# An attention block and a two-of-eight expert layer on one core: experts computed only on the rows routed to them, gathered and summed through DRAM

## The chip, the cores and the metric

The kernel runs on one core of one Trainium2 chip. Its engines are TensorE (PE in the profile, PEld for its weight loads), VectorE (DVE), ScalarE (ACT), GpSimd (POOL) and SyncE (SP). SP and ACT issue DMAs through hardware queues, POOL through a software queue. The metric is the time of the launch in device microseconds.

## The reference

All is float32. A linear attention with a polynomial sketch gives x, 4352 tokens of 128 values; a router picks two of eight experts for each token, and the output is the sum of the two experts' results, weighted by their gates.

```python
def phi(x):                                   # S1, S2: (8, 32)
    a = np.einsum('rd,bhsd->bhsr', S1, x); b = np.einsum('rd,bhsd->bhsr', S2, x)
    return np.einsum('bhsi,bhsj->bhsij', a, b).reshape(*x.shape[:-1], r * r)
kv = np.einsum('bhsf,bhsd->bhfd', phi(k), v); z = np.sum(phi(k), axis=2)
x = num / den                                 # num = phi(q) kv, den = phi(q) z; batch 4, heads 4, seq 1088
noisy_logits = x @ w_gate + np.log1p(np.exp(x @ w_noise)) * noise
top2 = np.argpartition(-noisy_logits, 2, axis=1)[:, :2]      # top2_w: softmax over the two
for e in range(E):                            # E = 8, w1[e]: (128, 1024), w2[e]: (1024, 128)
    for k in range(2):
        mask = top2[:, k] == e
        h = np.maximum(x[mask] @ w1[e], 0.0)
        out[mask] += top2_w[mask, k, None] * (h @ w2[e])
```

## The kernel before, in words

A batch has 1088 tokens, that is 8 tiles of 128 and a rest of 64; the rests of two batches share a tile. `attention(b)` loads k, v and q of a batch (SP), makes the keys (`key_values`: transposes at line 224, sketches at 191, the product on VectorE at 185, the sum over tokens at 240 and 242), lets POOL write each pair of heads of q twice (`twice`, line 256), and then works on two groups of four tiles: `queries` (transposes at 267, sketches at 272 and 273, products at 277, times the keys' sums at 286) and `router` (transposes of x at 305, logits at 310, some 30 small VectorE operations from 328 to 367). The router ends in the weight of every expert for every token, zero for six of eight. These weights are transposed on TensorE (371), stored to DRAM as (expert, token) by POOL (375) and read back spread over all partitions (395).

`experts` computes all eight experts for all 512 tokens of a group: x times the spread weight (398), w1 (402), ReLU on VectorE or ScalarE in turn (406, 408), w2 (389), all experts summed in one bank of PSUM. All weights, 8 MB, are loaded once (178, 179) and stay in SBUF. Then the sum is transposed back and stored (454, 456). There are eight groups of 512 tokens and one of 256, the rests. Batch 0's attention comes first; from then on each batch's attention is written ahead of the experts of two earlier groups.

The order on each engine is set when the kernel is built: a scheduler sorts the instructions of each engine, and attention's instructions stand between those of earlier groups' experts. Every engine takes its list in order. Tiles come from pools of a few buffers, and whoever writes a buffer waits until the last reader of its earlier content is done; a DRAM tile is one such object, so a write to it waits for the write before.

Of the kernel before, what the change touches and what calls it, by code (L numbers as in the profile page):

```python
# [16 lines left out]
# The largest float32 whose exp is finite.  # L17
# [4 lines left out]
def kernel(  # L22
# [22 lines left out]
    # A batch is NT full tiles of 128 tokens, token NT * p + t in row p of tile t, and a rest  # L45
    # of 64; the rests of two batches share a tile.
# [3 lines left out]
    G = 4  # L50
# [4 lines left out]

    const = ctx.enter_context(tc.tile_pool(name="const", bufs=1))
# [3 lines left out]
    keep = ctx.enter_context(tc.tile_pool(name="keep", bufs=2 * NG + 1))  # L60
    moe = ctx.enter_context(tc.tile_pool(name="moe", bufs=2))
    hpool = ctx.enter_context(tc.tile_pool(name="hpool", bufs=4))
    dram = ctx.enter_context(tc.tile_pool(name="dram", bufs=2 * NG + 1, space=DRAM))
# [50 lines left out]
    # Keys: rows (h, d), columns (h, sketch, r), a block for each head; the high and the low part.  # L114
# [6 lines left out]
    # Queries, for two heads: rows (part, h, d), columns (h, i, j), the i-th row of the first  # L121
    # sketch or the j-th of the second.
# [13 lines left out]
    # E for the first expert down to 1 for the last: of equal logits the first is taken.  # L136
# [26 lines left out]
    w1 = const.tile([P, E, F], F32, name="w1")  # L163
    w2 = const.tile([P, E, FJ, D], F32, name="w2")
# [12 lines left out]
    def load_weights(e):  # L177
        nc.sync.dma_start(w1[:, e, :], moe_w1[e])
        nc.sync.dma_start(w2[:, e, :, :], moe_w2[e].rearrange("(j p) d -> p j d", p=P))

# [119 lines left out]
    def router(x, n, t0):  # L300
        """x transposed, and every expert's weight of each token, in DRAM as (expert, token)."""
# [4 lines left out]
        xT = keep.tile([P, 512], F32, name="xT", tag="xT")  # L306
# [18 lines left out]
        # log(1 + exp(z)) = max(z, 0) + log(1 + u), u = exp(-|z|), with what 1 + u rounds off.  # L325
# [11 lines left out]
        # Where exp(z) overflows the reference's scale is infinite: one that outweighs all others.  # L337
# [6 lines left out]
        # The two largest, each one expert even among equals.  # L344
# [19 lines left out]
        gate = t3("gate")  # L364
        V.tensor_mul(out=gate, in0=first[0], in1=wide(g1))
        V.tensor_mul(out=c, in0=first[1], in1=wide(g2))
        V.tensor_add(out=gate, in0=gate, in1=c)  # L367
# [4 lines left out]
        gT = small.tile([E, 512], F32, name="gT", tag="gT")  # L372
        nc.vector.tensor_copy(gT[:, 0:w], ps[0:E, 0:w])
        gd = dram.tile([E, 512], F32, name="gd", tag="gd")
        nc.gpsimd.dma_start(gd[:, 0:w], gT[:, 0:w])
        return xT, gd

# [1 line left out]
    turn = [0]  # L379

    def experts(xT, gd, n):
        """The weighted experts of a group of tokens, as (token, D) in tiles of 128."""
        w = P * n
        acc = ps_o.tile([P, 512], F32, name="acc", tag="acc")
        EH = E // 4
        todo = []

        def second(e, j, h):
            nc.tensor.matmul(acc[:, 0:w], lhsT=w2[:, e, j, :], rhs=h[:, 0:w],  # L389
                             start=(e == 0 and j == 0), stop=(e == E - 1 and j == FJ - 1))  # L390

        for e0 in range(0, E, EH):
            # The weights are not negative: relu(w1 (g x)) = g relu(w1 x).
            gb = moe.tile([P, EH, 512], F32, name="gb", tag="gb")
            nc.gpsimd.dma_start(gb[:, :, 0:w], gd[e0:e0 + EH, 0:w].partition_broadcast(P))  # L395
            xg = moe.tile([P, EH, 512], F32, name="xg", tag="xg")
            for e in range(EH):
                nc.vector.tensor_mul(out=xg[:, e, 0:w], in0=gb[:, e, 0:w], in1=xT[:, 0:w])  # L398
            for e in range(e0, e0 + EH):
                for j in range(FJ):  # L400
                    hp = ps_h.tile([P, 512], F32, name="hp", tag="hp")
                    nc.tensor.matmul(hp[:, 0:w], lhsT=w1[:, e, P * j:P * (j + 1)],  # L402
# [8 lines left out]
                    if len(todo) > 2:  # L411
                        second(*todo.pop(0))
# [90 lines left out]
```

## Time and profile before

| | us |
|---|---|
| median of 2 runs (1117.38 to 1117.74) | 1117.56 |
| profiled execution, its span | 1118.2 |
| PE busy | 1066.1 |
| DVE busy | 327.1 |
| ACT busy | 230.8 |
| POOL busy | 46.4 |

The span runs from the first to the last instruction of one profiled execution. Busy times of different engines overlap. PE and PEld overlap as well, and a matmul's recorded duration is longer than the time by which it moves its successor, so rates are read from starts. A granted clock of 1.00 is TensorE's upper level, 2.4 GHz, and 0.50 the lower, 1.2 GHz.

### The profile page before, as it was taken

What the parts mean: (1) busy time and instruction counts of PE and PEld (TensorE: products, weight loads), DVE (VectorE), ACT (ScalarE), POOL (GpSimd) and SP (SyncE); (2) the same over time, 40 slices, a digit from 0 to 9 for tenths busy, and PEclk for the clock granted to TensorE, in tenths of its full rate; (3) what the DMA queues carried; (4) which work ended last, traced back from release to release, by engine and by line L of the source; (5) the groups of instructions that cost most, each with busy time, mean ns of one, the idle gap of its engine ahead of it and who ended that gap; (6) DMA issues with size and microseconds to landing.
All of it is one profiled execution on the core that took longest, in us unless ns stands there. A gap on an engine that the chain in (4) does not pass through costs nothing.

```text
span 1118.2 us, 8232 instructions
## 1 busy us (share of the span) xinstructions
PE 1066.1 (95%) x3072; PEld 535.6 (48%) x3072; DVE 327.1 (29%) x761; ACT 230.8 (21%) x406; POOL 46.4 (4%) x99
## 2 busy tenths in 40 slices
PE   1869999999999999999999999999999999999997
PEld 1636544444446444444455444444444444444586
DVE  2144442222223522222224522222223222222222
ACT  0123321111122311111113311111122111111221
POOL 2011100000000100000000000000000000000000
PEclk9969999999999999999999999999999999999999
DMA  8911000000000000000000000000000000000000
GB/s 209 317 45 51 21 1 23 26 25 27 22 24 5 20 19 19 28 20 19 20 29 0 21 20 19 29 19 19 19 29 19 19 20 28 10 10 10 19 1 6
DMA packets 29159, 35.95 MB, mean 32 GB/s; under 512 B 8056, under 2 KB 22656, under 8 KB 29120
## 3 DMA queue, kind: packets, MB, share of 16 engines
q1 hardware_dynamic: 17280, 16.91, 4.9%
q0 software_dynamic: 5216, 17.97, 4.8%
q10 hardware_dynamic: 6624, 0.56, 0.4%
q8 instruction: 24, 0.39, 0.1%
q14 instruction: 15, 0.12, 0.0%
HBM read 33.06 MB, written 2.37 MB: 32 GB/s over the span
## 4 chain that ended last, share of the span: by engine, by line
PE 89%; DVE 5%; DMA 2%; ACT 2%; issue 1%; ACTq 0%; POOL 0%; DVEq 0%
PE acc L389 39%; PE hp L402 39%; PE bank L272 2%; PE bank L240 2%; PE bank L191 2%; PE bank L273 1%; PE bank L286 1%; ACT L331 1%; PE bank L267 1%; DVE h L406 1%; PE bank L310 1%; DMA gb<-gd 1%; PE bank L371 0%; DMA words<-in_S_dram 0%; DMA rest_q<-in_q_dram 0%
## 5 line engine op out<-in xcount | busy, mean ns | idle before, releaser
L402 PE MATMUL hp<-xg,w 128*128 128x512 f32 (+1 forms) x1152 | 561.3, 569 | 0.0
L389 PE MATMUL acc<-h,w 128*128 128x512 f32 (+1 forms) x1152 | 558.7, 569 | 0.0
L406 DVE TENSOR_SCALAR h<-hp 128x512 f32<-128x512 f32 (+1 forms) x288 | 190.5, 662 | 608.9 <-PE hp L402 608.9
L389 PEld LDWEIGHTS acc<-h,w 128*128 128x128 f32 x1152 | 216.8, 190 | 235.4 <-issue 229.6
L402 PEld LDWEIGHTS hp<-xg,w 128*128 128x128 f32 x1152 | 215.9, 190 | 231.0 <-issue 227.7
L408 ACT ACTIVATE h<-hp 128x512 f32<-128x512 f32 (+1 forms) x288 | 165.0, 573 | 687.3 <-PE hp L402 687.3
L395 POOL DMA_DIRECT2D gb<-gd x36 | 20.1, 557 | 800.4 <-DVE xg L398 751.2
L398 DVE TENSOR_TENSOR xg<-gb,xT 128x512 f32<-128x512 f32 (+1 forms) x72 | 44.4, 654 | 2.4 <-DMA gb<-gd 2.4
L191 PE MATMUL bank<-sk,kT 128*128 128x64 f32 x136 | 20.1, 318 | 8.1 <-ACT kT L226 7.5
L277 DVE TENSOR_TENSOR phq<-qa,bank 128x512 f32<-128x512 f32 (+1 forms) x18 | 11.8, 658 | 44.6 <-PE bank L273 43.1
L191 PEld LDWEIGHTS bank<-sk,kT 128*128 128x128 f32 x136 | 19.9, 233 | 10.2 <-ACT kT L226 8.7
L272 PE MATMUL bank<-qT,sq 128*128 128x512 f32 (+1 forms) x36 | 21.8, 690 | 2.8 <-ACT qT L270 2.8
L286 PEld LDWEIGHTS bank<-kv,phq 128*128 128x128 f32 (+1 forms) x144 | 17.6, 186 | 9.4 <-DVE phq L277 4.0
L240 PE MATMUL bank<-vaug,phk 128*128 128x66 f32 x128 | 19.0, 311 | 3.0 <-DVE phk L185 3.0
L371 PE MATMUL bank<-ident,gate 128*8 128x128 f32 x34 | 5.6, 287 | 16.3 <-DVE gate L367 16.3
L240 PEld LDWEIGHTS bank<-vaug,phk 128*128 128x128 f32 x128 | 18.4, 226 | 5.0 <-DVE phk L185 3.2
L270 ACT COPY qT<-bank 128x512 f32<-128x512 f32 (+1 forms) x18 | 10.1, 562 | 49.7 <-PE bank L267 49.7
L273 PE MATMUL bank<-qT,sq 128*128 128x512 f32 (+1 forms) x36 | 20.0, 641 | 0.0
L286 PE MATMUL bank<-kv,phq 128*128 128x66 f32 (+1 forms) x144 | 17.2, 265 | 0.5 <-DVE phq L277 0.5
L185 DVE TENSOR_TENSOR phk<-kab 128x2048 f32<-128x2048 f32 x4 | 9.2, 2293 | 18.8 <-ACT kab L184 18.8
L205 PE MATMUL bank<-ident,rest_k 128*128 128x128 f32 x2 | 0.9, 446 | 14.3 <-DMA rest_k<-in_k_dram 14.3
L275 ACT COPY qa<-bank 128x512 f32<-128x512 f32 (+1 forms) x18 | 10.1, 562 | 19.5 <-PE bank L272 19.5
(98 smaller groups left out, 253.2 us busy)
## 6 DMA issues: line engine op xcount, KB each, us to landing
gb<-gd POOLq DMA_DIRECT2D x32, 512.0 KB, 3.9
w<-in_moe_w_dram SPq DMA_DIRECT2D x16, 512.0 KB, 7.7
kld<-in_k_dram SPq DMA_DIRECT2D x4, 512.0 KB, 6.5
vld<-in_v_dram SPq DMA_DIRECT2D x4, 512.0 KB, 6.9
qld<-in_q_dram SPq DMA_DIRECT2D x4, 512.0 KB, 5.6
out_dram<-y SPq DMA_DIRECT2D x8, 256.0 KB, 2.2
gb<-gd POOLq DMA_DIRECT2D x4, 256.0 KB, 3.6
words<-in_S_dram ACTq DMA_DIRECT2D x8, 2.0 KB, 4.7
```

Source lines behind the costliest of these rows:

```text
L191: nc.tensor.matmul(ps[:, c0:c0 + H * 2 * R], lhsT=kT, rhs=sk[:, i, :], start=(i == 0), stop=(i == 1))
L240: nc.tensor.matmul(o, lhsT=phk[:, t, hs, :].rearrange("p h f -> p (h f)"), rhs=vaug[:, hs, t, :], start=(t == 0), stop=False)
L272: nc.tensor.matmul(pa[:, 0:w], lhsT=sq[:, 0, :], rhs=qT[:, 0:w], start=True, stop=True)
L273: nc.tensor.matmul(pb[:, 0:w], lhsT=sq[:, 1, :], rhs=qT[:, 0:w], start=True, stop=True)
L277: nc.vector.tensor_mul(out=ph[:, 0:w], in0=qa[:, 0:w], in1=pb[:, 0:w])
L286: nc.tensor.matmul(ps[rows, c0:c0 + 2 * A1], lhsT=phq[hp][:, P * i + rows.start:P * i + rows.stop], rhs=kv[:, hp, :], start=True, stop=True)
L389: nc.tensor.matmul(acc[:, 0:w], lhsT=w2[:, e, j, :], rhs=h[:, 0:w], start=(e == 0 and j == 0), stop=(e == E - 1 and j == FJ - 1))
L395: nc.gpsimd.dma_start(gb[:, :, 0:w], gd[e0:e0 + EH, 0:w].partition_broadcast(P))
L398: nc.vector.tensor_mul(out=xg[:, e, 0:w], in0=gb[:, e, 0:w], in1=xT[:, 0:w])
L402: nc.tensor.matmul(hp[:, 0:w], lhsT=w1[:, e, P * j:P * (j + 1)], rhs=xg[:, e - e0, 0:w], start=True, stop=True)
L406: nc.vector.tensor_scalar_max(h[:, 0:w], hp[:, 0:w], 0.0)
L408: nc.scalar.activation(out=h[:, 0:w], in_=hp[:, 0:w], func=AF.Relu)
```

## The change

The router now keeps, in place of eight weights a token, which two experts were chosen and the two gates. Two small matmuls against a triangle and a matrix of ones give each (token, expert) pair its rank among the rows of its expert. The row of x times its gate, with the token's number as 129th value, is scattered to that expert's stretch of a DRAM tile `xs`, one indirect DMA on POOL for each tile and choice, 68 in all. When all tokens are routed, `table` works out on VectorE which blocks of rows there are: 27 blocks of 256 rows and 21 of 128, which is 75 times 128 rows for the 8704 pairs. `ends` writes padding behind each expert's last row. `blocks` goes through the 48 blocks: SP reads the expert's number and the first row into registers and fetches rows, w1 and w2 of that block (5 buffers); rows are transposed, w1, ReLU, and w2 with the hidden rows as stationary operand, so that results come out row by row; POOL adds them, by the token numbers, into a DRAM tile `total` that was cleared at the start. Before the last six blocks ACT copies `total` to `out`, and the rest is added into `out` itself.

```diff
-    w1 = const.tile([P, E, F], F32, name="w1")
-    w2 = const.tile([P, E, FJ, D], F32, name="w2")
...
+    moe = ctx.enter_context(tc.tile_pool(name="moe", bufs=3))
+    wpool = ctx.enter_context(tc.tile_pool(name="wpool", bufs=5))
...
+    def clear():
+        for r0 in range(0, N + P, 2 * P * 8):
+            n = min(2 * P * 8, N + P - r0)
+            nc.scalar.dma_start(total[r0:r0 + n, :].rearrange("(p r) d -> p (r d)", p=P),
+                                zeros[:, 0:n * D // P])
+        for c in range(2):
+            nc.scalar.dma_start(xs[E * CAP + P * c:E * CAP + P * (c + 1), :], pad[:])
...
-        for i in range(n):
-            nc.tensor.transpose(ps[0:E, P * i:P * (i + 1)], gate[:, i, :], ident[:])
-        nc.vector.tensor_copy(gT[:, 0:w], ps[0:E, 0:w])
-        nc.gpsimd.dma_start(gd[:, 0:w], gT[:, 0:w])
+        V.tensor_add(out=mk, in0=first[0], in1=first[1])
+        for i in range(n):
+            V.tensor_add(out=before[:, t0 + i + 1, :], in0=before[:, t0 + i, :], in1=masks[:, t0 + i, :])
+        nc.tensor.matmul(o, lhsT=earlier[:], rhs=mk.rearrange("p i e -> p (i e)"), start=True, stop=False)
+        nc.tensor.matmul(o, lhsT=ones[:], rhs=before[:, t0:t0 + n, :].rearrange("p i e -> p (i e)"),
+                         start=False, stop=True)
...
+        for i, g in enumerate((g1, g2)):
...
+            V.tensor_copy(to[:, 0:n], at)
+            nc.gpsimd.tensor_copy(xg[:, 0:n, D:XW].bitcast(I32), token[:, t0:t0 + n].unsqueeze(2))
+            V.tensor_tensor(out=xg[:, 0:n, 0:D], in0=x[:, 0:n, :, :].rearrange("p i h d -> p i (h d)"),
+                            in1=g.unsqueeze(2).to_broadcast([P, n, D]), op=ALU.mult)
+            for t in range(n):
+                nc.gpsimd.indirect_dma_start(
+                    out=xs[:], out_offset=bass.IndirectOffsetOnAxis(ap=to[:, t:t + 1], axis=0),
+                    in_=xg[:, t, :], in_offset=None)
...
+    def ends(tab):
+        for e in range(E):
+            at = 2 * (NB + NS) + e
+            r = nc.values_load(tab[0:1, at:at + 1], engines=SP, min_val=0, max_val=E * CAP - P,
+                               skip_runtime_bounds_check_because=IN_RANGE)
+            nc.sync.dma_start(xs[bass.ds(r, P), :], pad[:])
+
+    def fetch(tab, k, n):
+        e = nc.values_load(tab[0:1, 2 * k:2 * k + 1], engines=SP, min_val=0, max_val=E - 1,
+                           skip_runtime_bounds_check_because=IN_RANGE)
...
+        nc.sync.dma_start(xb[:, 0:n, :], xs[bass.ds(r, P * n), :].rearrange("(c p) d -> p c d", p=P))
+        nc.sync.dma_start(w1[:], moe_w1[bass.ds(e, 1), :, :].rearrange("o p f -> p (o f)"))
+        nc.sync.dma_start(w2[:], moe_w2[bass.ds(e, 1), :, :].rearrange("o (j p) d -> p (o j) d", p=P))
...
+        def second():
+            acc, h, w2, n, js, j0, xb, to = later.pop(0)
+            for i in range(js):
+                for c in range(n):
+                    j = j0 + i
+                    nc.tensor.matmul(acc[:, D * c:D * (c + 1)], lhsT=h[:, P * (n * i + c):P * (n * i + c + 1)],
+                                     rhs=w2[:, j, :], start=(j == 0 and c == 0), stop=(j == FJ - 1),
...
+            if j0 + js == FJ:
+                if to is out and not copied:
+                    copied.append(nc.scalar.dma_start(out, total[0:N, :]))
+                y = moe.tile([P, 2 * D], F32, name="y", tag="y")
+                evict(y[:, 0:D * n], acc[:, 0:D * n])
+                for c in range(n):
+                    nc.gpsimd.indirect_dma_start(
+                        out=to[:], out_offset=bass.IndirectOffsetOnAxis(ap=xb[:, c, D:XW].bitcast(U32), axis=0),
+                        in_=y[:, D * c:D * (c + 1)], in_offset=None, compute_op=ALU.add)
...
-    attention(0)
-    for b in range(1, B):
+    for b in range(B):
         attention(b)
-        for _ in range(NG):
-            expert_group(*groups.pop(0))
...
+    router(x, 2, B * NT)
+    tab = table()
+    ends(tab)
+    for i in range(max(NB, NS)):
+        order += [(i, 2)] * (i < NB) + [(NB + i, 1)] * (i < NS)
+    blocks(tab, order, copy_at=2 * NS)
```

How the lists of the engines change is shown at three places. A row is one instruction: line, operation, what it writes and reads, shape, and the semaphores that it waits for (DMASW are DMAs issued by POOL, DMAHW those of SP and ACT).

On POOL, where batch 0's first group is routed, the list before has one store of the weights, `gd`, and four loads `gb` that wait for a VectorE that is done with a buffer:

```order
L375 DMA gd<-gT 8x512 [waits DVE_49]
L395 DMA gb<-gd 128x1024 [waits DMASW0_49]
L256 COPY qx<-qld 128x8x64 [waits DMAHW5_49,PE_49,Pool_49]
L256 COPY qx<-qld 128x8x64 x3
L395 DMA gb<-gd 128x1024
L395 DMA gb<-gd 128x1024 [waits DMASW1_49,DVE_49]
L395 DMA gb<-gd 128x1024 [waits DMASW2_49,DVE_49]
```

At the same place POOL now has the eight scatters of the group (`xg_432` first choice, `xg_444` second):

```order
L433 DMA xs<-xg_432,to_430 36096x129 [waits DMAHW3_49,DMAHW4_49,DVE_49,Pool_49]
L300 COPY qx<-qld 128x8x64 [waits DMAHW5_49,PE_49,Pool_49]
L433 DMA xs<-xg_432,to_430 36096x129 [waits DMASW0_49]
L300 COPY qx<-qld 128x8x64 x3
L433 DMA xs<-xg_432,to_430 36096x129 [waits DMASW1_49]
L433 DMA xs<-xg_432,to_430 36096x129 [waits DMASW2_49]
L433 DMA xs<-xg_444,to_442 36096x129 [waits DMASW3_49,DVE_49,Pool_49]
L428 COPY xg_919<-token 128x4
L433 DMA xs<-xg_444,to_442 36096x129 [waits DMASW4_49]
L433 DMA xs<-xg_444,to_442 36096x129 [waits DMASW5_49]
L262 COPY kx<-kld 128x1024 [waits DMAHW0_49,PE_49,Pool_49]
L433 DMA xs<-xg_444,to_442 36096x129 [waits DMASW6_49]
```

Each scatter waits for the DMA that POOL issued before it, and copies that the next batches' attention needs (`qx`, `kx`) stand between and behind them.

On TensorE, from the router of batch 0's first group to the queries of its second, the list before ends the router with transposes of the weights, and expert matmuls (402) stand among the next group's queries:

```order
L310 MATMUL bank<-wgn,xT 128x16 x3
L371 MATMUL bank<-ident,gate 8x128 [waits DVE_49,PE_49]
L371 MATMUL bank<-ident,gate 8x128 x3
L267 MATMUL bank<-ident,qx 128x128 [waits PE_49]
L267 MATMUL bank<-ident,qx 128x128 x3
L272 MATMUL bank<-qT,sq 128x512 [waits Activation_49]
```

Now the two matmuls of the ranks are there, the second behind the next group's first transposes:

```order
L354 MATMUL bank<-wgn,xT 128x16 x3
L415 MATMUL bank<-masks,earlier 128x32 [waits DVE_49,PE_49]
L311 MATMUL bank<-ident,qx 128x128 [waits PE_49]
L311 MATMUL bank<-ident,qx 128x128 x3
L416 MATMUL bank<-before,ones 128x32 [waits DVE_49]
L316 MATMUL bank<-qT,sq 128x512 [waits Activation_49]
```

As before, TensorE goes on to the next group only when VectorE has finished the choice of experts (`masks` where it was `gate`); nothing of the experts stands between any two groups.

On POOL, at the end of the program, the list before has the last loads of weights:

```order
L395 DMA gb<-gd 128x1024 [waits DMASW5_49,DVE_49]
L395 DMA gb<-gd 128x1024 [waits DMASW6_49,DVE_49]
L395 DMA gb<-gd 128x2x256 [waits DMASW7_49,DMASW4_49,DVE_49]
L395 DMA gb<-gd 128x2x256 [waits DMASW0_49,DVE_49]
L395 DMA gb<-gd 128x2x256 [waits DMASW1_49,DVE_49]
```

Now it has the adds of the blocks' results, of which these are the last into `total` and the first into `out`:

```order
L568 DMA total<-y,xb 4480x128 [waits DMAHW7_49,DMASW7_49,DVE_49]
L568 DMA total<-y,xb 4480x128 [waits DMASW0_49]
L568 DMA total<-y,xb 4480x128 [waits DMAHW2_49,DMASW1_49,Activation_49]
L568 DMA out_dram<-y,xb 4352x128 [waits DMAHW5_49,DMAHW1_49,Activation_49]
L568 DMA out_dram<-y,xb 4352x128 [waits DMASW3_49]
L568 DMA out_dram<-y,xb 4352x128 [waits DMAHW0_49,DMASW4_49,Activation_49]
```

Here too each waits for POOL's DMA before it (DMASW), and for VectorE's or ScalarE's `y`; the first into `out` waits for ACT's copy (DMAHW1), which itself waits for the last into `total`.

## Rows read from the trace of the kernel before

**Rows 1.** The page: part 1, busy time by engine, and part 4, the chain by engine.

```profile
PE 1066.1 (95%) x3072; PEld 535.6 (48%) x3072; DVE 327.1 (29%) x761; ACT 230.8 (21%) x406; POOL 46.4 (4%) x99
...
PE 89%; DVE 5%; DMA 2%; ACT 2%; issue 1%; ACTq 0%; POOL 0%; DVEq 0%
```

**Rows 2.** Groups by line, shapes apart: count, busy us, mean ns, idle before.

```profile
L402 PE MATMUL hp<-xg,w 128*128 128x512 f32 x1024 | 523.4, 593 | 0.0
...
L402 PE MATMUL hp<-xg,w 128*128 128x256 f32 x128 | 37.9, 379 | 0.0
```

**Rows 3.** The chain in order of time: start us, us, what.

```profile
219.24 2.58 PE acc L389 x6
```

**Rows 4.** Timeline of PE near the end: start us, us, engine, line, operation.

```profile
1098.46 0.59 PE L389 MATMUL acc<-h,w 128*128 128x256 f32 x2
1098.89 0.59 PE L402 MATMUL hp<-xg,w 128*128 128x256 f32 x2
```

**Rows 5.** Timeline of PE, narrow matmuls in batches 0 and 1.

```profile
26.98 7.09 PE L191 MATMUL bank<-sk,kT 128*128 128x64 f32 x32 [7.55 <-ACT kT L226]
37.07 3.68 PE L240 MATMUL bank<-vaug,phk 128*128 128x66 f32 x16 [3.00 <-DVE phk L185]
...
95.85 1.04 PE L224 MATMUL bank<-ident,kx 128*128 128x128 f32 x8
97.58 3.68 PE L191 MATMUL bank<-sk,kT 128*128 128x64 f32 x32
...
104.59 1.90 PE L240 MATMUL bank<-vaug,phk 128*128 128x66 f32 x16
```

**Rows 6.** Timeline of PE in batch 0: key transposes, query transposes of both groups.

```profile
17.52 1.92 PE L224 MATMUL bank<-ident,kx 128*128 128x128 f32 x8
...
45.53 1.12 PE L267 MATMUL bank<-ident,qx 128*128 128x128 f32 x4
...
71.45 1.06 PE L267 MATMUL bank<-ident,qx 128*128 128x128 f32 x4
```

**Rows 7.** Timeline: POOL's first store and load of weights, SP's last stores.

```profile
72.68 0.67 POOL L375 DMA_DIRECT2D gd<-gT  x1 [26.53 <-DVE gT L373]
...
74.89 0.58 POOL L395 DMA_DIRECT2D gb<-gd  x1 [1.54 <-DMA gd<-gT]
...
1113.40 2.43 SPq L454 DMA_DIRECT2D out_dram<-y  x4
```

**Rows 8.** DMA issues: queue, count, KB each, median us to landing.

```profile
rest_q<-in_q_dram ACTq DMA_DIRECT2D x4, 32.0 KB, 5.1
...
gd<-gT POOLq DMA_DIRECT2D x8, 16.0 KB, 1.8
out_dram<-y SPq DMA_DIRECT2D x4, 32.0 KB, 1.9
```

**Rows 9.** Windows: stretch, its length, busy time of engines, PEclk, DMA share, GB/s.

```profile
37.00:45.00 8.00, 7.93 (x35) 7.56 (x35) 0.02 (x1) 0.00 (x0) 0.00 (x0) 1.00 1.12 341
45.50:70.70 25.20, 14.60 (x46) 8.46 (x46) 8.20 (x39) 6.34 (x11) 0.65 (x1) 0.78 0.40 123
1056.00:1112.00 56.00, 56.00 (x261) 48.75 (x259) 15.62 (x37) 12.78 (x33) 0.11 (x1) 1.00 0.03 10
```

**Rows 10.** Groups by line of VectorE, ScalarE and POOL, shapes apart.

```profile
L406 DVE TENSOR_SCALAR h<-hp 128x512 f32<-128x512 f32 x256 | 176.9, 691 | 568.5 <-PE hp L402 568.5
L408 ACT ACTIVATE h<-hp 128x512 f32<-128x512 f32 x256 | 152.8, 597 | 646.1 <-PE hp L402 646.1
...
L256 POOL COPY qx<-qld 128x512 f32<-128x512 f32 x16 | 9.7, 650 | 6.2 <-issue 6.2
...
L375 POOL DMA_DIRECT2D gd<-gT x9 | 4.9, 546 | 140.3 <-DVE gT L373 131.3 <-PE bank L224 9.0
...
L196 POOL COPY vaug<-vld 128x1024 f32<-128x1024 f32 x4 | 4.2, 1040 | 5.0 <-DMA vld<-in_v_dram 5.0
...
L353 DVE TENSOR_TENSOR first<-c,pick 128x32 f32<-128x32 f32 x16 | 3.0, 190 | 0.3
```

More of the change, by code (lines that the diff above doesn't have):

```diff
@@ L372, in router @@
-        gT = small.tile([E, 512], F32, name="gT", tag="gT")
-        nc.vector.tensor_copy(gT[:, 0:w], ps[0:E, 0:w])
-        gd = dram.tile([E, 512], F32, name="gd", tag="gd")
-        nc.gpsimd.dma_start(gd[:, 0:w], gT[:, 0:w])
-        return xT, gd
-    turn = [0]
[L381 to L402, printed above, removed]
-                                     rhs=xg[:, e - e0, 0:w], start=True, stop=True)
-                    h = hpool.tile([P, 512], F32, name="h", tag="h")
-                    if turn[0] % 2:
-                        nc.vector.tensor_scalar_max(h[:, 0:w], hp[:, 0:w], 0.0)
-                    else:
-                        nc.scalar.activation(out=h[:, 0:w], in_=hp[:, 0:w], func=AF.Relu)
-                    turn[0] += 1
-                    todo.append((e, j, h))
-                    if len(todo) > 2:
-                        second(*todo.pop(0))
-        for t in todo:
-            second(*t)
-        yT = moe.tile([P, 512], F32, name="yT", tag="yT")
-        nc.scalar.copy(yT[:, 0:w], acc[:, 0:w])
-        ps = bank()
-        for i in range(n):
-            nc.tensor.transpose(ps[:, P * i:P * (i + 1)], yT[:, P * i:P * (i + 1)], ident[:])
-        y = moe.tile([P, G, D], F32, name="y", tag="y")
-        nc.vector.tensor_copy(y[:, 0:n, :].rearrange("p i d -> p (i d)"), ps[:, 0:w])
-        return y
@@ new lines, in blocks @@
+    def blocks(tab, order, copy_at):
+        later, copied = [], []
+        def second():
[5 more added lines that the diff above has]
+                                     rhs=w2[:, j, :], start=(j == 0 and c == 0), stop=(j == FJ - 1),
+                                     skip_group_check=True)
+            if j0 + js == FJ:
[3 more added lines that the diff above has]
+                evict(y[:, 0:D * n], acc[:, 0:D * n])
+                for c in range(n):
+                    nc.gpsimd.indirect_dma_start(
+                        out=to[:], out_offset=bass.IndirectOffsetOnAxis(ap=xb[:, c, D:XW].bitcast(U32), axis=0),
+                        in_=y[:, D * c:D * (c + 1)], in_offset=None, compute_op=ALU.add)
+        data = [fetch(tab, *order[0])]
+        xTs = [block_input(data[0][0], order[0][1])]
+        for s_, (k_, n) in enumerate(order):
+            xb, w1, w2 = data.pop(0)
+            xT = xTs.pop(0)
+            if s_ + 1 < len(order):
+                data.append(fetch(tab, *order[s_ + 1]))
+            acc = ps_o.tile([P, 2 * D], F32, name="acc", tag="acc")
+            js = 4 // n
+            for j0 in range(0, FJ, js):
+                hp = ps_h.tile([P, 512], F32, name="hp", tag="hp")
+                for i in range(js):
+                    nc.tensor.matmul(hp[:, P * n * i:P * n * (i + 1)], lhsT=w1[:, P * (j0 + i):P * (j0 + i + 1)],
+                                     rhs=xT[:, 0:P * n], start=True, stop=True)
+                h = hpool.tile([P, 512], F32, name="h", tag="h")
+                evict(h[:], hp[:], relu=True)
+                later.append((acc, h, w2, n, js, j0, xb, out if s_ >= copy_at else total))
+                if len(later) > 2:
+                    second()
+                if j0 + 2 * js == FJ and s_ + 1 < len(order):
+                    xTs.append(block_input(data[0][0], order[s_ + 1][1]))
+        while later:
+            second()
@@ L440, in attention @@
             key_rests()
-            for e in range(E):
-                load_weights(e)
+            clear()
         kvs.append(key_values(b, kld, vld))
```

156 lines of the change are left out of this document (130 added, 26 removed).

## The prediction

> **What bounds the kernel now.** I read the page's first part and the summary of the chain that ended last, then the groups by line, then the pieces of the chain, then the timeline at four places. The reader is to see in [rows 1] that TensorE is busy 95% of the span and carries 89% of the chain: nothing but its own work sets the end. [rows 2] says which work: the expert matmuls of line 402, 1024 instructions of 512 columns and 128 of 256; line 389 has as many of each. A float32 matmul is issued as two passes, so 1024 instructions are 512 matmuls. Six passes of 512 columns take 2.58 us [rows 3], so 430 ns a pass; two of 256 columns start 0.43 us after the two before them [rows 4], so 216 ns. The experts are 2048 x 0.430 + 256 x 0.216 = 936 us of a span of 1118.2 us. The median of the runs shown is 1117.56 us, 0.6 us under that span, which I neglect. What is left, 182 us, is the start, where batch 0's attention runs alone, and the later batches' matmuls between those of the experts.
>
> **The change, step by step. TensorE's expert work.** The new kernel does 27 blocks of 256 rows and 21 of 128. Per big block: 8 first-layer matmuls of 256 columns (16 passes) and 16 second-layer matmuls of 128 (32 passes); per small one 16 and 16 passes of 128 columns. No row shows a float32 pass of 128 columns that is no transpose. From above it is bounded by 216 ns, the 256-column pass, from below by the narrow passes with new weights each: 3.68/32 = 115 ns at 64 columns and 1.90/16 = 119 ns at 66 [rows 5], which barely depend on columns. Half of 216 is 108, so I take 110. A big block costs 16 x 0.216 + 32 x 0.110 = 7.0 us and two transposes at 1.04/8 = 0.13 us [rows 5], so 7.2; a small one 32 x 0.110 + 0.13 = 3.65. All blocks: 27 x 7.2 + 21 x 3.65 = 271 us in place of 936. The evictions are 75 x 2 of 512 columns at 0.6 to 0.7 us [rows 10] on two engines, and hide.
>
> **Attention loses its cover, and is now a stage of its own.** TensorE's list shows that nothing of the experts stands between two groups any more. I read its length from batch 0, which ran alone: from one group's query transposes to the next group's, 71.45 - 45.53 = 25.9 us [rows 6]; the added mask matmul waits for VectorE where the gate transpose did, so 26. Keys: 1.9 us of transposes [rows 6], 7.1 for line 191 and 8.5 from line 240's first instruction at 37.07 [rows 5] to the query transposes, and about 4 us of copies and products between, 21.5 in all. A batch is 73.5 us. In batch 0 line 191 starts at 27.0 us [rows 5]; ACT has five clearing DMAs ahead of the copy that it waits for, so 31; 18.5 us later queries, two groups: 101.5. Three more batches: 322. The group of rests, about 20: 342. These rows are at the lower clock: the same 32 passes took 7.09 us there and 3.68 later [rows 5]; the granted clock of the stretch 45.5 to 70.7 is recorded as 0.78 and that of the end as 1.00 [rows 9] (1.00 stands for 37 to 45 too, where passes were as slow; I go by the passes). At the upper level a batch would lose some 20 us, the stage 80.
>
> **The scatter of routed rows.** 68 indirect DMAs of 128 rows each, and POOL's list shows that every one waits for the one before to land, with the copies for the next batch behind them. The trace has no indirect DMA. From below: POOL is busy 0.55 us with a plain store [rows 10] and it lands 1.8 us later [rows 8], so 2.35 us a link; the one case where a DMA waited for such a store has 74.89 - 72.68 = 2.2 us [rows 7]. From above: the small rest loads, issued while the queues were full, took 5.1 us [rows 8], 5.65 a link. Queues are nearly idle in this stage, so I stay near the lower end: 3.0, as 128 rows are described by index instead of 8 in order. Eight links per group are 24 us against 26 of attention, so the scatter keeps pace until 4.1 us a link (16 links and 4.7 us of POOL's copies, four of line 256, one of line 196 and one of its size for `kx` [rows 10], against 73.5). The last full group is ready at 322 + 3.5, its eight links end at 349.5, four for the rests at 361.5. VectorE's table, some 63 small operations at 0.19 us [rows 10], is over at about 357 and hides behind them; with faster links it would show.
>
> **Row ends and the first block.** Eight stores of padding on SP, each waiting for the last: 0.6 us of issue, as SP needed 2.43 us for four [rows 7], and 1.9 of landing [rows 8], so 20 us: 381.5. The first block's rows and weights take 4.5 more: 386. SP's register loads of row numbers appear nowhere in the trace: below nothing, above the 5.66 us a block (271/48) from which fetching would bind; I take them as hidden, since five blocks are buffered. Weights fetched 48 times are 50 MB, rows 5 MB, and the adds move some 15 MB: 70 MB. The weight loads ran at 341 GB/s [rows 9], so 205 us, under 271.
>
> **The scatter-adds.** 75 links in a row again, each adding 64 KB into DRAM, on the same POOL chain and the same bounds, 2.35 and 5.65 us. The target is read first, and weights stream beside it at some 200 of 341 GB/s, so I take the middle, 4.0 us. That is above TensorE's 3.6 us for 128 rows (7.2 + 3.65 for three links), so the links bind, narrowly: three make 12.0 us against 10.85. Blocks of xb are freed only when their add has landed, and y has three buffers, so TensorE and ACT fall into step. First add at 394.5; 63 adds into `total` end at 646.5. Then ACT copies 2.2 MB from `total` to `out`: by 341 GB/s, read and written, 13 us; nothing covers it, the twelve last adds wait for it. 659.5, and 12 x 4.0 = 48: 707.5, plus 2 for the end: **710 us**.
>
> The nearest row gave a link of 2.2 to 2.3 us without load. The Trainium skill, DMA: Bandwidth & Descriptors, "Anatomy of one DMA — SWDGE (gpsimd) path", fits a DMA from this engine as 2.0 us plus its bytes over 436 GB/s, mostly the receipt of the write, and the rules for kernel authors there say to merge transfers under 64 KB. An estimate by that page is 2.15 us and POOL's 0.55, so 2.7 a link; by it the links never bind and the sum would be some 670. That page also says that an accumulating DMA must be waited for before another touches the same bytes, which is what the list does.
>
> **Rivals.** (a) Adds under 3.6 us: TensorE binds. 386 + 21 x 10.85 + 7.2 = 621 at the end of the first block of `out`, 13 for the copy, 12 links of 3.5, 2: **680 us**. For it: the unloaded link of 2.2 us [rows 7]. Against it: the weights beside it and the read of the target.
> (b) Links of 5 to 6.8 us: 5.65 gives 394.5 + 75 x 5.65 + 15 = **833 us**. For it: the 5.1 us of the rest loads [rows 8]; against it, those stood behind full queues.
> (c) TensorE stays at the lower clock in the blocks, because it waits in each of them. Passes double as line 191's did [rows 5]: a pair 21.7, so 386 + 21 x 21.7 + 14.4 + 5 x 14.4 + 10 = **940 us**. Against it: the 256-column passes at the end ran at 1.00 for 56 us [rows 9]. The Trainium skill, TensorE: Matmul & The Clock Gate, Part 1, says that an idle TensorE falls to half its clock and that sustained matmuls lift it; the rows of batch 0 agree with the first.
> (d) The other side: POOL's links are so long that they set both stages. First link at 49.5 + 26 + 3.5 = 79, then 143 links and 62 us that nothing hides (POOL's copies 14, ends 20, first block 13, copy and end 15): 141 + 143 p. It is slower than before from p = 6.9 us on; 8 us gives **1285 us**. For it: the trace has no indirect DMA that would bound p. Against it: the rest loads' 5.1 us [rows 8] is the longest median among its small transfers.
> (e) Attention at the upper clock, 80 us less of it, with (a): 600 us, or up to 630 where the scatter then sets the stage.
>
> **How the numbers follow.** Forecast, links of 3.6 to 5: 0.50, its own range 660 to 780. (a) 0.24, (b) 0.11, (c) 0.06, (d) 0.03, (e) 0.06. The predicted time is the likeliest's, 710. From 620 to 850 lie the forecast, (a), most of (b) up to 5.7 and part of (e), about 0.83. Over 2% is what a measurement of this kernel can tell: faster 0.96 (all but (d) and a part of (c) with long links), same 0.01, slower 0.03.
>
> **What would show it.** TensorE's 128-column passes at 108 to 120 ns; attention's groups 26 us apart and the first block's matmul near 386; the scatter's mean link near 3.0 and the add's near 4.0, with POOL's waits put down to its own DMAs; a hole in ACT of the adds' lag and about 13 us before the last twelve adds. It is wrong if SP's register loads release TensorE, if the table is later than the last scatter, or if a link is far from 4 us: one us there moves the end by 75.

## The result and the profile after

The changed kernel takes 800.61 us (799.43 to 801.78, 2 runs) where the kernel before took 1117.56 us: a ratio of 0.716, with a 95% interval of 0.713 to 0.719. That is inside the range of 620 to 850 us, 90 us above the forecast of 710 and outside the forecast's own 660 to 780. The span of the profiled execution is 800.1 us; all places below are in it.

The page's part 1 and its two groups of indirect DMAs (part 5: count, busy us, mean ns, idle before and what ended it):

```profile
PE 498.1 (62%) x2781; PEld 422.4 (53%) x2781; DVE 192.4 (24%) x664; ACT 119.1 (15%) x232; POOL 212.6 (27%) x233
...
L568 POOL DMA_INDIRECT total<-y,xb x63 | 98.1, 1557 | 296.8 <-issue 108.3
...
L433 POOL DMA_INDIRECT xs<-xg,to x68 | 68.3, 1005 | 169.0 <-DMA xs<-xg,to 80.7
```

TensorE was busy 95% of the span before [rows 1] and is now busy 62%. No engine fills the span any more. What fills it is found from stretch to stretch. The same windows as in [rows 9] for the new stages (length, busy time of each engine, granted clock, DMA share, GB/s):

```profile
101.00:336.00 235.00, 141.12 (x537) 104.73 (x536) 87.65 (x399) 46.20 (x82) 70.55 (x88) 0.57 0.05 17
372.00:440.00 68.00, 54.26 (x395) 50.50 (x394) 13.91 (x24) 10.89 (x24) 19.39 (x13) 1.00 0.58 139
440.00:700.00 260.00, 183.42 (x1234) 166.24 (x1234) 43.87 (x75) 34.34 (x75) 69.39 (x45) 0.97 0.58 144
```

Attention lasts to about 320 us at a granted clock of 0.57, the lower level for most of the time. In the blocks the clock is the upper one, and TensorE is busy for 70 to 80% of a stretch.

**First stage and what joins it to the blocks.** Timeline rows (start us, us, engine, line, operation, and in brackets the idle time before and what ended it) of PE, POOL and SP:

```profile
48.15 1.11 PE L311 MATMUL bank<-ident,qx 128*128 128x128 f32 x4
...
71.20 1.09 PE L311 MATMUL bank<-ident,qx 128*128 128x128 f32 x4
...
319.32 0.58 PE L415 MATMUL bank<-masks,earlier 128*128 128x16 f32 x2 [6.59 <-DVE g L407]
...
356.57 0.66 PE L545 MATMUL bank<-ident,xb 128*128 128x128 f32 x2 [35.64 <-DMA xb<-xs]
```

```profile
311.86 0.96 POOL L433 DMA_INDIRECT xs<-xg,to  x1 [1.74 <-DMA xs<-xg,to]
314.40 0.96 POOL L433 DMA_INDIRECT xs<-xg,to  x1 [1.59 <-DMA xs<-xg,to]
```

```profile
338.86 13.65 SPq L518 DMA_DIRECT2D xs<-pad  x8
354.23 0.42 SPq L526 DMA_DIRECT2D xb<-xs  x1
```

A group of attention takes 71.20 - 48.15 = 23.05 us here, and 25.25 us at most elsewhere. A scatter with the wait for its landing takes 314.40 - 311.86 = 2.54 us where nothing else holds it up (median of all 2.7), so eight are done in some 20 to 22 us and the scatters keep pace. Then TensorE has nothing to do for 35.6 us: the last scatters, the eight stores of padding one behind the other, and the fetch of the first rows.

**The adds.** POOL's timeline where the blocks run evenly. The rows are the two adds of a big block, the add of a small one, and the two of the next big block:

```profile
387.73 1.55 POOL L568 DMA_INDIRECT total<-y,xb  x1 [4.87 <-issue]
394.43 1.56 POOL L568 DMA_INDIRECT total<-y,xb  x1 [5.15 <-DMA total<-y,xb]
398.34 1.55 POOL L568 DMA_INDIRECT total<-y,xb  x1 [2.35 <-ACT y L539]
405.18 1.56 POOL L568 DMA_INDIRECT total<-y,xb  x1 [5.29 <-issue]
411.92 1.55 POOL L568 DMA_INDIRECT total<-y,xb  x1 [5.18 <-DMA total<-y,xb]
```

From start to start these links take 6.70, 3.91, 6.84 and 6.74 us: two long ones, one short, and so on to the end of the stage. The short one is that behind the second add of the big block, at 394.43. The 63 adds into `total` start from 372.42 to 730.83, a mean link of 358.4 / 62 = 5.78 us. POOL itself works 1.56 us in each; the rest is a wait for the landing, whatever name stands in the bracket ("issue" is time in which nothing that the profile shows was waited for, and `y` was itself late for want of a buffer that an earlier add held).

What is different at the long ones is seen on SP's queue in the same stretch:

```profile
387.03 0.38 SPq L526 DMA_DIRECT2D xb<-xs  x1
387.92 0.34 SPq L529 DMA_DIRECT2D w<-in_moe_w_dram  x1
388.52 0.37 SPq L530 DMA_DIRECT2D w<-in_moe_w_dram  x1
397.64 0.34 SPq L526 DMA_DIRECT2D xb<-xs  x1
...
```

A fetch starts 0.7 us ahead of the adds at 387.73 and 398.34 (its two loads of weights follow the rows within 1.5 us), and none beside the one at 394.43. The waits of SP, POOL and TensorE in two stretches say why (us in total, times, longest; the first row from 380 to 640 us, the others from 372 to 731):

```profile
SPq L526 <- DMA total<-y,xb: 200.3, 33, 12.1
...
POOL total L568 <- issue: 108.3, 21, 6.4
POOL total L568 <- DMA total<-y,xb: 103.0, 21, 5.6
...
PE bank L545 <- DMA xb<-xs: 63.2, 37, 2.3
```

SP's fetch waits for a buffer of `xb`, and that is released when the last add of an older block has landed. The same landing lets POOL start the next add. So 1 MB of weights and the add set out together, in every block; only the second add of a big block has no fetch beside it, because the first one's landing frees nothing. TensorE then waits for rows.

**The end.** POOL's and ACT's timelines:

```profile
730.83 1.56 POOL L568 DMA_INDIRECT total<-y,xb  x1 [2.49 <-issue]
747.88 1.55 POOL L568 DMA_INDIRECT out_dram<-y,xb  x1 [15.50 <-issue]
...
793.30 1.56 POOL L568 DMA_INDIRECT out_dram<-y,xb  x1 [1.92 <-DMA out_dram<-y,xb]
```

```profile
736.94 0.58 ACTq L564 DMA_DIRECT2D out_dram<-total  x1
```

The copy of `total` holds POOL from 736.94 to 747.88, and the twelve last adds take 4.1 us each (45.4 us from the first start to the last, 11 links), with few weights left to load.

### The profile page after: what moved, and what is told of

The parts are those of the page before. It is cut to its first block, busy times and chain, and to the rows that moved or that the text cites. A ratio compares the mean times of both kernels' runs of the same rounds, so it can differ in the third digit from the quotient of the medians.

```text
span 800.1 us, 8013 instructions
## 1 busy us (share of the span) xinstructions
PE 498.1 (62%) x2781; PEld 422.4 (53%) x2781; DVE 192.4 (24%) x664; ACT 119.1 (15%) x232; POOL 212.6 (27%) x233
## 3 DMA queue, kind: packets, MB, share of 16 engines
q0 software_dynamic: 12976, 9.42, 7.6%
## 5 line engine op out<-in xcount | busy, mean ns | idle before, releaser
L584 PE MATMUL hp<-bT,w 128*128 128x256 f32 (+1 forms) x768 | 165.2, 349 | 35.3 <-DMA w<-in_moe_w_dram 34.1
L568 POOL DMA_INDIRECT total<-y,xb x63 | 98.1, 1557 | 296.8 <-issue 108.3
L559 PE MATMUL acc<-w,h 128*128 128x128 f32 x1200 | 164.1, 282 | 16.1 <-ACT h L539 16.1
L559 PEld LDWEIGHTS acc<-w,h 128*128 128x128 f32 x1200 | 160.2, 198 | 22.5 <-ACT h L539 16.5
L584 PEld LDWEIGHTS hp<-bT,w 128*128 128x128 f32 x768 | 120.8, 200 | 48.1 <-issue 24.3
L433 POOL DMA_INDIRECT xs<-xg,to x68 | 68.3, 1005 | 169.0 <-DMA xs<-xg,to 80.7
L537 DVE TENSOR_SCALAR h<-hp 128x512 f32<-128x512 f32 x80 | 55.3, 692 | 232.6 <-PE hp L584 231.4
L545 PE MATMUL bank<-ident,xb 128*128 128x128 f32 x75 | 18.8, 310 | 98.9 <-DMA xb<-xs 98.9
L539 ACT ACTIVATE h<-hp 128x512 f32<-128x512 f32 x70 | 41.8, 597 | 227.8 <-PE hp L584 205.4
L568 POOL DMA_INDIRECT out_dram<-y,xb x12 | 18.7, 1555 | 43.8 <-issue 26.3
```

Of the source, the lines that this page charges most:

```text
L433: nc.gpsimd.indirect_dma_start(out=xs[:], out_offset=bass.IndirectOffsetOnAxis(ap=to[:, t:t + 1], axis=0), in_=xg[:, t, :], in_offset=None)
L537: nc.vector.tensor_scalar_max(o, i, 0.0) if relu else nc.vector.tensor_copy(o, i)
L539: nc.scalar.activation(out=o, in_=i, func=AF.Relu) if relu else nc.scalar.copy(o, i)
L545: nc.tensor.transpose(ps[:, P * c:P * (c + 1)], xb[:, c, 0:D], ident[:])
L559: nc.tensor.matmul(acc[:, D * c:D * (c + 1)], lhsT=h[:, P * (n * i + c):P * (n * i + c + 1)], rhs=w2[:, j, :], start=(j == 0 and c == 0), ...
L568: nc.gpsimd.indirect_dma_start(out=to[:], out_offset=bass.IndirectOffsetOnAxis(ap=xb[:, c, D:XW].bitcast(U32), axis=0), in_=y[:, D * c:D * ...
```

## Experiments

What was to be told apart: are the long links made by the weights that stream beside the add, by the add itself, by POOL and its queue, or by the moment at which the fetch is released? Where a mean link is given below it is worked out from the starts of the first and the last of the 63 adds into the sum; the three medians are those of the links behind the first and the second add of a big block and the add of a small one, from the eighth link on. The runs given without an interval are single executions; the two of the changed kernel above are 2.4 us apart.

**Weights fetched once.**

```diff
     def fetch(tab, k, n):
...
+        if len(held_w) == 5:
+            held_w.append(held_w.pop(0))
+            return (xb,) + held_w[-1]
         w1 = wpool.tile([P, F], F32, name="w1", tag="w1")
```

> Weights are fetched for the first five blocks only and used again by the blocks behind them (so the sums are taken with other experts' weights; the work on every engine but the transfers stays). Collision theory: two links of three between adds are long (6.7 us) because the landing of an add releases the next fetch, whose 1 MB of weights stands ahead of the next add; with no weights all links are the short one, 4.0 us: 372.4 + 63 x 4.0 = 624, + 17 to the first add to the output + 12 x 4.0 + 7 = 696 us (685 to 710). Rival, the add's own landing: the long links are a property of the add (read and add in DRAM, big and small blocks unlike), the weights have no part: 800 us, links still 6.8, 6.7 and 4.0. Rival, POOL or the issuing engines: no change either, 800 us.

Measured: 681.0 us, 4 us under the expected 685 to 710: the links came as expected, but from the last of them to the first add into `out` there were 9 us, where 17 were allowed. POOL's timeline and the page's group of the adds:

```profile
398.46 1.55 POOL L574 DMA_INDIRECT total<-y,xb  x1 [2.02 <-DMA total<-y,xb]
402.54 1.56 POOL L574 DMA_INDIRECT total<-y,xb  x1 [2.53 <-ACT h L545]
406.51 1.55 POOL L574 DMA_INDIRECT total<-y,xb  x1 [2.41 <-DVE h L543]
410.18 1.56 POOL L574 DMA_INDIRECT total<-y,xb  x1 [2.11 <-DMA total<-y,xb]
```

```profile
L574 POOL DMA_INDIRECT total<-y,xb x63 | 98.1, 1557 | 184.6 <-issue 55.3
```

The links are short: 4.08, 3.97, 3.67 here, a mean of (616.88 - 370.74) / 62 = 3.97, and 58 of the 62 are under 4.5 (four take 5.2 to 6.1). POOL's 1.557 us an add is unchanged to the nanosecond; its idle time fell by 112 us, and the kernel by 120. What makes the long links long is the weights, not POOL and not the add, which by itself takes 3.97 us of the 5.78.

**Half the weights.** Only w2 is fetched after the fifth block.

```diff
+        if len(held_w) == 5:
+            held_w.append(held_w.pop(0))
+            w1 = held_w[-1]
+        else:
+            w1 = wpool.tile([P, F], F32, name="w1", tag="w1")
...
         nc.sync.dma_start(w2[:], moe_w2[bass.ds(e, 1), :, :].rearrange("o (j p) d -> p (o j) d", p=P))
```

> From the sixth block on only the second weights are fetched (0.5 MB a block), the first ones are used again from the first five blocks (so the sums are taken with other experts' first weights). If the long links come from bytes that stream while the add is under way, the excess falls with them, from 2.75 us to about half: links 5.4, 5.4, 4.0, 42 x 1.35 = 57 us less, 745 us (725 to 765). If any large fetch beside an add costs the same, whatever its size, 800 us; the run with twice the weights, in which long links grew by 0.4 us alone, would speak for this one.

Measured: 747.5 us, as the first theory had it; medians 5.13, 4.04 and 5.64, mean 4.94.

**Twice the weights.**

```diff
+        v1 = wpool.tile([P, F], F32, name="v1", tag="v1", bufs=3)
+        v2 = wpool.tile([P, FJ, D], F32, name="v2", tag="v2", bufs=3)
+        nc.sync.dma_start(v1[:], moe_w1[bass.ds(e, 1), :, :].rearrange("o p f -> p (o f)"))
+        nc.sync.dma_start(v2[:], moe_w2[bass.ds(e, 1), :, :].rearrange("o (j p) d -> p (o j) d", p=P))
```

> Every block loads both weights a second time, into buffers that nobody reads: 2 MB behind each fetch in place of 1 MB, nothing else changed. Collision theory: the long links grow by what 1 MB takes, about the 2.8 us by which they now exceed the short ones: 42 x 2.8 = 118, so 920 us (880 to 950), the short links stay at 4.0. Rival, the add's own landing: links as they are, 800 to 815 us. Rival, POOL: 800 us.

Measured: 831.9 us, 88 us short of the first theory's number and outside its bounds. The medians are 7.37, 4.08 and 7.27, the mean 6.19. Set side by side, with the time of the kernel:

| weights beside an add, MB | first of big | second of big | small | mean link | us |
|---|---|---|---|---|---|
| 0 | 3.55 | 4.02 | 4.02 | 3.97 | 681.0 |
| 0.5 | 5.13 | 4.04 | 5.64 | 4.94 | 747.5 |
| 1 (the changed kernel) | 6.63 | 4.05 | 6.80 | 5.78 | 800.6 |
| 2 | 7.37 | 4.08 | 7.27 | 6.19 | 831.9 |

Up to 1 MB a long link grows by about 2.9 us per MB; the second MB costs 0.6 us more (the 0.4 in two of the expectations is the growth of the mean of all links, long and short). POOL's and SP's timelines of this run show that the add does not wait for all that was asked for:

```profile
497.48 1.56 POOL L572 DMA_INDIRECT total<-y,xb  x1 [2.52 <-ACT y L543]
504.73 1.55 POOL L572 DMA_INDIRECT total<-y,xb  x1 [5.70 <-issue]
```

```profile
499.02 0.43 SPq L533 DMA_DIRECT2D v<-in_moe_w_dram  x1
499.64 0.38 SPq L534 DMA_DIRECT2D v<-in_moe_w_dram  x1
504.02 0.38 SPq L526 DMA_DIRECT2D xb<-xs  x1
```

The add that began at 497.48 had landed by 504.02, when the next fetch was released, though the last of the four loads asked for at 499.64 takes some 7 us to land in this run (page, part 6, 7.3 us for `v`). So the theory "an add waits behind all weights of its fetch" fell, and the smaller claim stands: an add beside a stream of weights takes up to about twice as long (7.37 against 3.55 us and 7.27 against 4.02). If the packets share the DMA engines in turn, or if an add waits only for what was asked for before its own packets, the table could bend like this.

**Late weights.** Meant to tell these two apart.

```diff
+        for i in range(2):
+            late = wpool.tile([1, 16], F32, name="late", tag="late", bufs=1)
+            nc.sync.dma_start(late[:], moe_w1[0:1, 0, 0:16])
         w1 = wpool.tile([P, F], F32, name="w1", tag="w1")
```

> Between a block's rows and its weights SP's queue now loads 64 bytes twice into one small tile; the second load waits for the first to land, so the weights are asked for some 2.5 to 3 us later than now, behind the 1.56 us in which POOL writes the add's descriptors and not ahead of their end. Nothing else is changed, the same 1 MB a block is moved. Order theory: an add is held by what stands in the DMA queues before its own packets, and not by what comes behind them (this would be why a second MB added only 0.4 us): long links fall to 4.0 to 4.7, 720 us (700 to 745). Sharing theory: transfers under way slow each other whichever was first; the weights still stream while the add's packets are on their way, and later adds meet the late weights too: links 5.5 to 6.8, 775 to 810 us.

Measured: 799.75 us, ratio 0.715 (0.713 to 0.716) to the kernel before, links 6.56, 4.04 and 6.74. But SP's timeline shows that the edit did not do what it was for:

```profile
493.32 0.38 SPq L526 DMA_DIRECT2D xb<-xs  x1
494.23 0.35 SPq L532 DMA_DIRECT2D w<-in_moe_w_dram  x1
494.82 0.37 SPq L533 DMA_DIRECT2D w<-in_moe_w_dram  x1
495.25 4.84 SPq L529 DMA_DIRECT2D late<-in_moe_w_dram  x2
```

The scheduler put the small loads behind one fetch and ahead of the next one's rows, where SP waits anyway; the weights are asked for 0.9 us after the rows, as without the edit. The run itself says nothing on the order of packets.

The packets that the traces keep do. In the changed kernel POOL's work on the add at 387.73 ends at 389.28. What the DMA engines moved from then to 391.90 us, and from there to the landing (queue, packets, MB, share of 16 engines; q0 is POOL's queue, q1 the one that brings rows and weights):

```profile
q1 hardware_dynamic: 594, 0.70, 85.7%
```

```profile
q1 hardware_dynamic: 574, 0.29, 43.2%
q0 software_dynamic: 144, 0.07, 23.5%
```

For 2.6 us weights alone are moved and not one packet of the add; then its 144 packets pass beside the rest. The same as medians over the adds with a fetch beside them, from the eighth add on (in the first row, over all adds of the run with weights fetched once):

| weights beside an add, MB | POOL's end to the add's first packet, us | first to last packet, us |
|---|---|---|
| 0 | 0.57 | 0.8 |
| 0.5 | 1.8 to 1.9 | 1.1 |
| 1 (the changed kernel) | 2.8 to 3.0 | 1.4 to 1.5 |
| 2 | 2.5 to 3.1 | 1.9 to 2.0 |

So a long link is for the most part a wait of the add's packets until most of the weights asked for before them have passed. With 2 MB that wait is no longer, and there the second MB was asked for only when POOL had done its part (the `v` at 499.02, POOL's end at 499.04; 0.4 us behind it in the median); it slows the packets, not their start. That fits the order theory, with sharing for what comes later, and does not fit turns taken from the start. It is read from the traces; no run moved the weights behind the add to try it.

**Plain scatter, no add.**

```diff
-                        in_=y[:, D * c:D * (c + 1)], in_offset=None, compute_op=ALU.add)
+                        in_=y[:, D * c:D * (c + 1)], in_offset=None)
```

> The results are scattered without adding (each row of the sum holds only the last of what was written to it; the sum is left out). The 75 links remain, one behind the other. Collision theory: a link falls only by what the add costs more than the plain scatter of the first stage, 4.0 - 2.54 = 1.5 us, two of three still stand behind weights (5.3 us): mean 4.4, 372.4 + 63 x 4.4 + 16 + 12 x 2.6 + 7 = 704 us (690 to 720). Rival, the add's own landing: with no add no long link is left, 2.5 us each, and TensorE binds at 356.6 + 271, so about 650 to 665 us.

Measured: 697.6 us; medians 4.81, 2.96 and 5.12, mean (641.0 - 371.82) / 62 = 4.34. The pattern of two long and one short stays where nothing is added, so it does not come from adding. The add costs 1.1 us more than a plain scatter where no weights stream, of which POOL has 0.6:

```profile
L568 POOL DMA_INDIRECT total<-y,xb x63 | 60.3, 957 | 243.7 <-DMA total<-y,xb 83.3
```

**More buffers.**

```diff
-        xb = wpool.tile([P, 2, XW], F32, name="xb", tag="xb")
+        xb = wpool.tile([P, 2, XW], F32, name="xb", tag="xb", bufs=10)
...
-                y = moe.tile([P, 2 * D], F32, name="y", tag="y")
+                y = moe.tile([P, 2 * D], F32, name="y", tag="y", bufs=6)
```

> Ten input buffers in place of five, and six for the results in place of three; one sum, every add still waits for the one before. The fetches are then no longer started by an add's landing, but by the weights' buffers, which TensorE frees. If only the coincidence of trigger and add made links long, they move apart and most links fall to 4.0: 690 to 720 us. If an add is slow whenever weights stream beside it, whoever starts them, the 48 MB are still to be brought within the same 360 us, long links lose their fixed place among the three but not their number: mean link 5 to 6, 770 to 805 us.

Measured: 796.9 us, which can't be told from the 800.6 of the changed kernel, with a mean link of 5.87. SP's waits from 380 to 640 us are still those for an add's landing, only later by some blocks, and the first seven links, before the buffers are full, are all long (4.76 to 7.67 us). SP's waits, then two of the first adds:

```profile
SPq L526 <- DMA total<-y,xb: 164.5, 27, 9.5
```

```profile
377.17 1.59 POOL L568 DMA_INDIRECT total<-y,xb  x1 [6.06 <-DMA w<-in_moe_w_dram]
384.10 1.56 POOL L568 DMA_INDIRECT total<-y,xb  x1 [5.35 <-ACT y L539]
```

With the chain of adds slower than TensorE, ten buffers fill as five did, and then the oldest add's landing paces the fetch again (medians 6.29, 4.03, 7.22). So the common trigger does not look like the root. It places the collisions, and even spares one link of three; in the seven links without it the weights met the adds all the same.

**Two sums.** Adds go to two DRAM sums in turn and wait for the add before the last one; the two are added at the end through SBUF, in place of the copy.

```diff
+    totals = [dram.tile([N + P, D], F32, name=f"total{i}", tag=f"total{i}") for i in range(TOTALS)]
...
+                    to = totals[len(copied) % TOTALS]
+                    copied.append(c)
...
+                (nc.sync, nc.scalar)[(i + t) % 2].dma_start(part[:], r[:, cs])
...
+                nc.vector.tensor_add(out=parts[0][:], in0=parts[0][:], in1=part[:])
+            (nc.sync, nc.scalar)[i % 2].dma_start(o[:, cs], parts[0][:])
```

> Adds go to two sums in turn, so that each waits only for the add two before it; the two are added at the end by way of SBUF in four pieces, in place of the copy to the output. Chain theory (the serial wait for the landing is what costs, whatever lengthens it): two links may overlap, 5.8 / 2 = 2.9 us an add, below TensorE's 10.85 / 3 = 3.6; TensorE binds: 356.6 + 21 x 10.85 + 6 x 7.2 = 628, + 10 to the last landing, + 20 to 25 for the sums: 660 us (645 to 685). Rival, the queue itself is the limit (POOL's queue or the add's memory traffic takes 5.8 us per add, waited for or not): 372 + 75 x 5.8 + 25 = 830 us, no faster than now.

Measured: 672.2 us, ratio 0.601 (0.599 to 0.603) to the kernel before. A window in the blocks and POOL's timeline:

```profile
440.00:636.00 196.00, 196.00 (x1462) 187.92 (x1461) 53.14 (x88) 40.67 (x88) 83.89 (x54) 1.00 0.84 213
```

```profile
507.49 1.56 POOL L570 DMA_INDIRECT total<-y,xb  x1 [3.31 <-DVE y L539]
509.36 1.55 POOL L570 DMA_INDIRECT total<-y,xb  x1 [0.30 <-issue]
```

TensorE is busy for 196 of 196 us at the upper clock. Adds start 1.87 us apart where two results are ready, beside more GB/s than before (213 against 144): the queue takes them. Each still takes 5.7 us to land in the median of this window (6.0 in the changed kernel). What cost the time was one add waiting for another, at a price that the weights raised.

**Two sums, shorter end.** The same, with the end in eight pieces and loads four pieces ahead.

```diff
-            for part in parts[1:]:
-                nc.vector.tensor_add(out=parts[0][:], in0=parts[0][:], in1=part[:])
...
+        for i in range(AHEAD):
+            load_parts(i)
+        for i in range(PIECES):
+            a, b = parts[i]
+            nc.vector.tensor_add(out=a[:], in0=a[:], in1=b[:])
```

> Two sums as in the run with two sums, the last addition of the two in eight pieces with their loads four pieces ahead of the stores, in place of four pieces two ahead. Chain theory: all but the end as there, TensorE without a pause from 372 to 640 us; the end moved 6.6 MB in 27.7 us with a hole of 9 us before the third piece, so about 6 us less: 666 us (660 to 672). Rival, the end is bound by the transfers themselves: 672 us.

Measured: 668.9 us (666.5 to 671.6), ratio 0.598 (0.595 to 0.600). The runs of the two overlap (669.6 to 674.6 us with four pieces) and the gain is half of what was expected. In the two profiled executions the stretch from the last add's start to the end shrank from 29.1 to 26.1 us; that it is now bound by the transfers of 6.6 MB is not ruled out. It is 132 us under the changed kernel.

## Why the prediction was right, and where it was not

The sign and, in kind, the mechanism came as forecast: TensorE's expert work shrinks by more than two thirds, attention becomes a stage of its own, scatters keep pace with it, and in the blocks the serial adds bind and TensorE does not. The time did not come as forecast. Links of 3.6 to 5 us were its condition, and a link far from 4 us was named as a sign of its being wrong; they take 5.78, and 800.6 us lies outside its 660 to 780. The wider range holds the result because it takes in most of rival (b). One term was 112 us too small, and by luck a first add that came 22 us early hid a part of it:

| term | predicted us | measured us | from |
|---|---|---|---|
| first add starts | 394.5 | 372.4 | timeline of POOL |
| first to last add landed in `total` | 252 | 364.5 | 736.94 - 372.42 |
| copy | 13 | 10.9 | 747.88 - 736.94 |
| twelve adds to `out`, and the end | 50 | 52.2 | 800.1 - 747.88 |
| sum | 710 | 800.1 | |

**TensorE's passes: right.** Four passes of 256 columns and eight of 128 follow in 1.76 us (this PE timeline, of the changed kernel near its end): with 0.216 a pass of 256 [rows 4], (1.76 - 0.86) / 8 = 0.112 us against the 0.110 that I took.

```profile
745.78 1.03 PE L584 MATMUL hp<-bT,w 128*128 128x256 f32 x4
746.65 1.05 PE L559 MATMUL acc<-w,h 128*128 128x128 f32 x8
747.54 1.03 PE L584 MATMUL hp<-bT,w 128*128 128x256 f32 x4
```

The sum of 271 us for all blocks is seen where nothing holds TensorE, in the run with two sums, whose blocks run from 364.7 to 639.2 us: 274.5.

**Attention, scatter and ends: right in kind, 29 us too long, of which the first block gave 7 back.** A group takes 23.05 to 25.25 us where I read 26 from batch 0 of before [rows 6], and a batch 66.7 to 69.0 where I had 73.5 (its first query transposes stand at 48.15, 116.97, 183.71 and 252.67 us), so the group of rests starts at 301.1 and not at 322. In that stretch of before the DMA engines were 0.40 busy with the weights [rows 9], and in the same stretch now they are 0.07 busy; that this is the reason was not tried. The scatter's link is 2.54 to 2.7 us where I took 3.0 between 2.35 and 5.65. The ends take 354.23 - 338.86 = 15.4 us, not 20. So the first block's transposes come at 356.57 in place of 386. The first add follows 15.9 us later and not 8.5, which I had not seen coming: TensorE waits 2.3 us for the first weights, and after its 35.6 idle us the granted clock is 0.50, the lower level, from 356.5 to 364.7 us. The low clock of this stage came as forecast (0.57 from 101 to 336 us), so rival (e) fell; the upper clock of the blocks (0.97 to 1.00) disposes of rival (c).

**The add's link: the step that failed.** I took 4.0 us, "the middle" of 2.35 and 5.65, for an add with weights beside it, and it is 5.78. Two mistakes are in that step. The lower bound was a plain store's, and an add without any weights already takes 3.97 us, by the first experiment: POOL alone has 1.56 us where the store had 0.55 [rows 10]. And I weighed the stream of weights by its average, "some 200 of 341 GB/s", as if it slowed an add a little. The stream is not spread out: 1 MB comes in a burst, and at most adds a burst is under way, which costs 2.9 us there. The argument against rival (b), that the 5.1 us of the rest loads [rows 8] "stood behind full queues", was the argument for it: the DMA engines are 0.88 busy from 5 to 25 us of before, where those loads stand, and 0.86 busy behind the add shown above (389.28 to 391.90 us). In its size the measured link belongs to rival (b), 5 to 6.8 us. The time is 33 us under its 833: 22 from the early first add, and the rest mainly because the last twelve links take 4.1 us each.

**Rival (a)** could not come with one sum: the link without weights, 3.97 us, is still above TensorE's 3.6. It came when the wait was taken away, by the two sums, at 672 us for the 680 that I gave it; that the numbers are so near is in part luck, as the blocks began some 20 us sooner and the end is another one. **Rival (d)** needed links of 6.9 us in both stages; the scatter's are 2.54.

**The skill's figure.** The Trainium skill, DMA: Bandwidth & Descriptors, "Anatomy of one DMA — SWDGE (gpsimd) path", gave an estimate of 2.7 us a link. The plain scatter of the first stage, 2.54 us, agrees with it. The add does not: 3.97 us alone and 5.78 beside weights, so the measurement decides, and the 670 us that followed from the page did not come with one sum.

**What would have shown it in the trace of before.** Only the bounds: nothing in it adds into DRAM. But the changed program showed that the fetch waits for a buffer that an add frees, as the prediction says itself, and that the next add waits for the same landing. From "two things start together, one of them 1 MB" follow the rows for small transfers beside full queues, not those for idle ones.

## What to carry to other kernels

A chain of DMAs that each wait for the one before costs its latency times its length, whatever its bytes; take the wait away first (two targets in turn took 128 us off here), before buffers are added, which the chain here only filled. Price a small transfer by the rows with the queues in the state in which it will find them: ask which event releases it, and what else that event releases. An average GB/s says nothing of a burst that starts at the same moment.

## What the hardware showed that I had not expected

- An indirect DMA of 128 rows of 512 bytes costs POOL 0.96 us when it writes and 1.56 us when it adds; part 3 of the page counts 12976 packets in POOL's queue for all 143 of them, and 4576 when the 75 do not add, so 112 more for each add (144 in place of 32). By the traces an add's 64 KB go in 128 packets of 512 bytes, a plain scatter's in 16 of 4096.
- An add into DRAM takes 3.97 us from start to start with no weights beside it. Where no fetch stands beside either, it takes 4.05 us and the scatter of the same rows 2.96.
- 1 MB of weights beside it adds 2.9 us, a second MB only 0.6 us more. Most of the 2.9 us is a wait until the add's first packet moves, which the second MB, asked for later, did not lengthen (2.5 to 3.1 us against 2.8 to 3.0).
- Two adds from the same queue to different targets overlap: they start 1.87 us apart, and TensorE at 1.00 of its clock is then the limit.
